# Attention and two gated layers on one core: ten zero products in front, the first pair's last keys in a bank of the fold's, w_out's first piece requested ahead of the first values

## The chip, the cores and the metric

The kernel runs on one core of a Trainium2 chip. The metric is the device time of one execution in microseconds; a time of a kernel is the median of its runs. TensorE (PE in the profile; PEld is its weight loads), VectorE (DVE), ScalarE (ACT), GpSimd (POOL) and SyncE (SP, which requests most transfers) work side by side, each through its own list of instructions in order.

## The reference

Three layers follow each other, without a non-linearity between the second and the third's first product:

```python
scores = cap * np.tanh(scale * np.matmul(q, k.transpose(0, 1, 3, 2)) / cap)
attn = np.exp(scores - np.max(scores, axis=-1, keepdims=True))
attn = attn / (np.sum(attn, axis=-1, keepdims=True) + 1e-09)
x = np.matmul(attn, v)                 # 4 batches, 12 heads, 448 tokens, 64 wide
...
h = (x @ w1) * (x @ w2) @ w3 @ w_out   # 1792 x 768, 768 x 1024, 1024 x 1024, 1024 x 768
...
h = h @ w_in                           # 768 x 1024
e = np.exp(h - h.max(-1)); solu = h * e / (e.sum(-1) + 1e-09)
out = ((solu - mean) / np.sqrt(var + 1e-06) * g_ln) @ w_out2
```

The weights of the second and third layer arrive in 64-bit floats; q, k, v and the weights as the kernel multiplies them are 32 bits wide.

## The kernel before

Two heads make a pair; there are 24 pairs, numbered from 0. A pair's 448 keys are cut into four chunks: chunks 0 to 2 of 128 keys for each head, and chunk 3, "the last keys", 64 keys of both heads in one. `scores` (L237) multiplies keys by queries into a PSUM tile of two banks, tag `sc0` or `sc1`, one buffer each; `exps` (L254) applies tanh in place and exp into SBUF (tile `p`) on ScalarE; `values` (L276) multiplies `p` by the values into the two banks of `o`. Pair 0 is scored with plain 32-bit products (two passes of an instruction for each half of the operands); from pair 1 on queries and keys are split by `split_pair` (L210) into a rounded part and a rest (`qh`, `ql`, `kh`, `kl`) on VectorE and scored in three products. The values of pairs 0 to 3 are used whole.

Beside this runs the *fold*: w3 @ w_out @ w_in is multiplied out once (`fold`, L368), first w_out by w3 (tile `f`, two buffers, tag "f"; L378). Its operands come through `Ahead` (L51): a list of pieces of 512 KB, each requested on SyncE (`landing`, L150, three landing buffers `ld`), turned from 64 to 32 bits in three VectorE operations (`convert`, L163: L168, L169, L170, into one of two buffers `cv`), and split by a ScalarE cast (L174) and a VectorE subtraction (L175). A landing buffer is free when the third operation has read it. The first pieces are w_out's chunk 0 in two halves (`in_wo`, tile `w_o_0`), then four of w3 (`in_w3t`; `w_0_0` to `w_0_3`), then w_out's chunks 1 to 5 in halves.

At the start (L655 to L679) SyncE requests the cap, then pair 0's queries, keys and values (`load_pair`, L189), then as many pieces as there are landing buffers, then pair 1's queries, keys and values. TensorE has nothing to multiply yet; `WARM` = 12 products of a tile of zeros (L663) fill the time, into a bank of tag "f". In the first turn of the loop over pairs (g = 0, phase 0) pair 0's chunks 0 and 1 are scored into `sc0` and `sc1`; six more zero products follow (L701); the last keys are scored into `sc0` again, once chunk 0's exponential has read it. The loop takes the chunks' exponentials in the order of L708:

```python
for turn, x in enumerate((run[0], (n + phase, 3), run[1])):
```

that is chunk 0, last keys, chunk 1. `ahead.step` (L719) puts the next piece's conversion beside them. The order in which instructions then stand on each engine is made by a scheduler from the program's order, priorities and its own estimate of times; on the chip each engine follows its list and waits where an operand isn't there. Names of the trace leave out pair numbers: `sc_3` or `p_3` of the order rows is chunk 3, `o_0` and `o_1` are the heads, a further number is a buffer's.

Of the kernel before, what the change touches and what calls it, by code (L numbers as in the profile page):

```python
# [10 lines left out]
F32 = mybir.dt.float32  # L11
# [8 lines left out]
P = 128  # L20
B, H, S, D = 4, 12, 448, 64
# [5 lines left out]
HALF = 512  # L27
# [8 lines left out]
NV = 2 * (NCH - 1) + 1  # L36
FILL = 4600
W3 = 9
WARM = 12
LANDS = 3  # L40
PASSES = ((0, 1), (2, 3))
NOP = 9
# [8 lines left out]
class Ahead:  # L51
# [9 lines left out]
    def loads(self):  # L61
        while self.loaded < len(self.items) and self.loaded < self.at + self.depth:
            _, load, _, _, _, there = self.items[self.loaded]
            if there is not None and not there():
                return
            load()
            self.loaded += 1

    def step(self, n=1):

# [28 lines left out]
def attention_moe_solu(ctx: ExitStack, tc: tile.TileContext, q, k, v, cap, w12, w3t, wo, win, wout2, g_ln, out):  # L99
# [9 lines left out]
    pe, act, dve, pool, sync = nc.tensor, nc.scalar, nc.vector, nc.gpsimd, nc.sync  # L109
# [34 lines left out]
    ps = ps_cm.__enter__()  # L144


    ahead = Ahead(LANDS)
# [38 lines left out]

    landed, ready, parts, outs, xr, stored, inv = {}, {}, {}, {}, {}, set(), [None]

    def load_pair(n):  # L189
        if n == 1:  # L190

            kd, qd = (at.tile([P, 2, S], F32, tag="hi", bufs=4, name=f"{x}d{n}").rearrange("p a s -> p (a s)")[:, :w] for x, w in (("k", HALF), ("q", S)))
        else:
            qd = at.tile([P, S], F32, tag="qd", name=f"qd{n}")
            kd = at.tile([P, HALF], F32, tag="kd", name=f"kd{n}")
        for t, src in ((qd, q), (kd, k)):
            sync.dma_start(out=t, in_=src[n])
        if n in PLAIN:
            vd = at.tile([P, 2, S], F32, tag="lo", bufs=4, name=f"vf{n}").rearrange("p a b -> p (a b)")
            vd = vd[:, :NV * (D + 1)].rearrange("p (c d) -> p c d", c=NV)  # L200
            pool.memset(vd[:, :, D:], 1.0)
            sync.dma_start(out=vd[:, :, :D], in_=v[n])
        else:
            vd = at.tile([P, NV, D], F32, tag="vd", name=f"vd{n}")
            sync.dma_start(out=vd, in_=v[n])
        landed[n] = qd, kd, vd
        if not n:
            ready[0] = qd, None, kd, None, vd
# [26 lines left out]
    tiled = [None, None]  # L235

    def scores(n, c, place_):  # L237

        qh, ql, kh, kl = ready[n][:4]
        sc = ps.tile([P, 2, HALF], F32, tag=f"sc{place_}", name=f"sc{n}_{c}")  # L240
        terms = ((kh, ql), (kl, qh), (kh, qh)) if n else ((kh, qh),)
        for m, (kk, qq) in enumerate(terms):
            keys = kk[:, c * P:(c + 1) * P]
            if c == 3:
                pe.matmul(sc[:, 0, :S], keys, qq, start=(m == 0), stop=(m == len(terms) - 1))
                continue
            for j in range(2):
                rows = slice(j * D, (j + 1) * D)
                tiled[0] = pe.matmul(sc[:, j, :S], keys[rows], qq[rows, :], start=(m == 0), stop=(m == len(terms) - 1))  # L249
        return sc  # L250
# [402 lines left out]


    sync.dma_start(out=capt, in_=cap.to_broadcast([P, 1]))  # L655
    load_pair(0)
    if WARM:

        zero = at.tile([P, 2, S], F32R, tag="hi", bufs=4, name="zero")
        dve.memset(raw(zero[:, 0]), 0.0)  # L660
        idle = ps.tile([P, HALF], F32, tag="f", bufs=2, name="idle")
        for i in range(WARM):
            pe.matmul(idle[:, :S], zero[:, 0, :P], zero[:, 0], start=True, stop=True)  # L663
# [25 lines left out]
    for g in range(NP // 2):  # L689
        n, first, at_once = 2 * g, g % 2, 2 * g in PLAIN  # L690
        for phase in range(3):
            run = (((n, 0), (n, 1)), ((n, 2), (n + 1, 0)), ((n + 1, 1), (n + 1, 2)))[phase]
            one, two = (first, 1 - first) if phase != 1 else (1 - first, first)
            with tc.high_priority():
                tiles = [scores(*run[0], one)]
                with tc.issue_after(tiled[0].ins):
                    tiles.append(scores(*run[1], two))
            if not g and not phase:
                with tc.issue_after(tiled[0].ins):
                    for i in range(WARM // 2):  # L700
                        pe.matmul(idle[:, :S], zero[:, 0, :P], zero[:, 0], start=True, stop=True)  # L701
            if phase:
                last_keys(n + phase - 1)
            if not at_once and (phase or n > len(PLAIN)):
                if not phase:
                    tiled[1] = tiled[0]
                behind(*(((n - 1, 1), (n - 1, 2)), ((n, 0), (n, 1)), ((n + 1, 0),))[phase])
            for turn, x in enumerate((run[0], (n + phase, 3), run[1])):  # L708
                if turn == 1:
                    if phase == 2:  # L710
                        continue
                    with tc.high_priority():
                        sc = scores(*x, one)
                else:
                    sc = tiles[turn // 2]
                split_scores(*x, exps(*x, sc))
                if g or phase:
                    with tc.issue_after(exp_[0, 1].ins) if not g else nullcontext():
                        ahead.step(2 if g >= NP // 4 else 1)  # L719
# [37 lines left out]
    ps = ps_cm.__enter__()  # L757
# [116 lines left out]
    a = operands(0)  # L874
# [3 lines left out]
    for n in range(PAIRS):  # L878
# [5 lines left out]
        if not last:  # L884
            a = operands(n + 1)
            if n + 2 < PAIRS:
                load_ab(n + 2)
        else:
            load_wg(1)
            a = turned_operands(0, tps)  # L890
# [7 lines left out]
    for n in range(PAIRS):  # L898
# [5 lines left out]
        if not last:  # L904
            a = turned_operands(n + 1, tps)
# [58 lines left out]
```

## Time and profile before

| | |
|---|---|
| median of 3 runs | 836.03 us (836.0 to 838.24) |
| the profiled execution | 837.27 us, its span 835.5 |
| TensorE busy, of the span | 819.0 us, 98% |
| VectorE, ScalarE, GpSimd | 586.2 (70%), 478.4 (57%), 74.8 (9%) |
| weight loads | 682.9 us (82%) |
| moved by DMA | 173.48 MB, mean 208 GB/s |

Instructions of one line of the kernel, engine and operand names form a group; a time in brackets at the end of a timeline's row is how long the engine had been idle before it, with what ended that. TensorE's busy time holds some waiting, since the products' ends are modelled: where a stretch is of interest, its products' starts are to be compared. Times are counted from the span's start.

### The profile page before, as it was taken

To read this page: it belongs to the slowest core of one execution; us is meant where nothing else is said; L and a number is where in the kernel's file an instruction comes from. 1 tells how busy PE (TensorE), PEld (TensorE's weight loads), DVE (VectorE), ACT (ScalarE), POOL (GpSimd) and SP (SyncE) were. 2 spreads that over 40 slices of the span, in tenths; PEclk is the share of its full clock that TensorE was granted. 3 is DMA by queue.
4 is the path that set the end of the run, shared out by engine and by line. 5 is a ranking of instruction groups with operands and counts; after the bars stand their busy time and mean duration, and the time that the engine had idled before them with its cause. 6 is when DMAs were issued, how large, how long until landed. Compare 5 with 4: busy or idle time off the path is not lost.

```text
span 835.5 us, 12215 instructions
## 1 busy us (share of the span) xinstructions
PE 819.0 (98%) x4363; PEld 682.9 (82%) x4363; DVE 586.2 (70%) x1048; ACT 478.4 (57%) x739; POOL 74.8 (9%) x149
## 2 busy tenths in 40 slices
PE   8999999999999999999899999999999999999998
PEld 4657888866777888887779899998888888999997
DVE  6889968878875787778855452433987877995452
ACT  6767868778677877765752220212555656763341
POOL 1110110110311221111111000000000000000000
PEclk9999999999999999999999999999999999999999
DMA  7878645578977355688677999983533325844211
GB/s 239 273 240 275 209 150 157 175 222 280 277 263 206 114 183 184 207 269 274 198 232 259 347 381 346 360 287 102 184 113 115 100 101 186 264 156 152 89 64 75
DMA packets 95645, 173.48 MB, mean 208 GB/s; under 512 B 13280, under 2 KB 66272, under 8 KB 93536
## 3 DMA queue, kind: packets, MB, share of 16 engines
q1 hardware_dynamic: 90592, 161.51, 57.5%
q0 software_dynamic: 4992, 11.19, 5.4%
q8 instruction: 34, 0.56, 0.3%
q14 instruction: 27, 0.22, 0.1%
HBM read 116.40 MB, written 50.68 MB: 200 GB/s over the span
## 4 chain that ended last, share of the span: by engine, by line
PE 70%; DVE 11%; DMA 11%; ACT 4%; issue 3%; SPq 0%; POOL 0%; DVEq 0%; POOLq 0%; ACTq 0%
PE ab L604 20%; PE u L766 16%; PE v L766 8%; PE o L290 6%; PE f L396 6%; PE f L378 5%; PE y L766 4%; DMA wg_dr<-cv 3%; PE sc L249 3%; DVE cv L169 2%; DMA ld<-in_wo 2%; DVE cv L170 2%; PE tp L836 1%; DVE cv L168 1%; DVE lo L273 1%
## 5 line engine op out<-in xcount | busy, mean ns | idle before, releaser
L604 PE MATMUL ab<-xs,wt 128*128 128x448 f32 x1152 | 241.7, 366 | 2.5 <-DVE abs L612 1.6
L604 PEld LDWEIGHTS ab<-xs,wt 128*128 128x128 f32 x1152 | 216.0, 188 | 23.9 <-DVE abs L612 2.0
L257 ACT ACTIVATE sc<-sc,qscale 128x896 f32<-128x896 f32 (+1 forms) x96 | 84.9, 884 | 34.8 <-PE sc L249 26.4
L258 ACT ACTIVATE p<-sc,capt 128x896 f32<-128x896 f32 (+1 forms) x96 | 85.6, 916 | 1.5
L290 PE MATMUL o<-hi,v 128*66 128x448 f32 (+1 forms) x360 | 84.7, 371 | 0.8 <-ACT x L306 0.6
L766 PE MATMUL u<-ws,a 128*128 128x512 f32 x336 | 82.1, 394 | 0.0
L378 PEld LDWEIGHTS f<-w,w_o 128*128 128x128 f32 x576 | 72.7, 191 | 10.5 <-issue 5.9
L378 PE MATMUL f<-w,w_o 128*128 128x256 f32 x576 | 78.5, 289 | 1.4 <-DVE w_o L175 0.9
L766 PEld LDWEIGHTS u<-ws,a 128*128 128x128 f32 x336 | 62.8, 187 | 14.8
L273 DVE TENSOR_TENSOR lo<-p,hi 128x896 fp32r<-128x896 f32 x60 | 64.9, 1084 | 9.7 <-ACT hi L269 9.5
L396 PE MATMUL f<-w_i,w 128*128 128x512 f32 x288 | 70.2, 393 | 1.1 <-DVE w L175 0.8
L608 ACT COPY a<-ab 128x448 f32<-128x448 f32 x32 | 17.0, 532 | 88.4 <-PE ab L604 84.1
L766 PE MATMUL u<-wg,c 128*128 128x384 f32 x336 | 65.4, 340 | 0.0
L396 PEld LDWEIGHTS f<-w_i,w 128*128 128x128 f32 x288 | 53.7, 188 | 14.3 <-DVE w L175 1.2
L168 DVE TENSOR_SCALAR cv<-ld 128x512 uint32<-128x512 uint32 (+1 forms) x80 | 32.8, 413 | 41.8 <-DMA wg_dr<-cv 25.3
L290 PEld LDWEIGHTS o<-hi,v 128*66 128x66 f32 (+1 forms) x360 | 39.1, 135 | 26.1 <-issue 9.1
L766 PEld LDWEIGHTS u<-wg,c 128*128 128x128 f32 x336 | 58.3, 188 | 0.1
L269 ACT CAST hi<-p 128x896 fp32r<-128x896 f32 x60 | 56.6, 947 | 0.4
L612 DVE TENSOR_TENSOR abs<-ab,a 128x448 f32<-128x448 f32 x32 | 19.9, 621 | 48.5 <-PE ab L604 41.3
L169 DVE SCALAR_TENSOR_TENSOR cv<-ld,cv 128x512 uint32<-128x512 uint32 (+1 forms) x80 | 52.1, 659 | 0.8
L170 DVE SCALAR_TENSOR_TENSOR cv<-ld,cv 128x512 uint32<-128x512 uint32 (+1 forms) x80 | 52.1, 658 | 0.7
L290 PE MATMUL o<-lo,v 128*66 128x448 f32 x120 | 42.6, 367 | 2.4 <-DVE lo L273 2.3
(132 smaller groups left out, 1237.4 us busy)
## 6 DMA issues: line engine op xcount, KB each, us to landing
ld<-in_w SPq DMA_DIRECT2D x24, 512.0 KB, 4.3
w_dr<-wt SPq DMA_DIRECT2D x8, 1536.0 KB, 6.5
wt<-w_dr SPq DMA_DIRECT2D x8, 1536.0 KB, 8.8
ld<-in_w3t SPq DMA_DIRECT2D x16, 512.0 KB, 4.4
ab_dr<-abs SPq DMA_DIRECT2D x32, 224.0 KB, 4.9
ldab<-ab_dr SPq DMA_DIRECT2D x14, 512.0 KB, 3.9
c_dr<-e SPq DMA_DIRECT2D x14, 512.0 KB, 2.6
ldc<-c_dr SPq DMA_DIRECT2D x14, 512.0 KB, 3.6
```

The source lines that it names most:

```text
L168: dve.tensor_scalar(x, hi, 5, 2, ALU.logical_shift_left, ALU.logical_shift_right)
L169: dve.scalar_tensor_tensor(x, hi, 0xC0000000, x, ALU.bitwise_and, ALU.bitwise_or)
L170: dve.scalar_tensor_tensor(x, lo, 29, x, ALU.logical_shift_right, ALU.bitwise_or)
L257: act.activation(sc[:, :w, :S], sc[:, :w, :S], AF.Tanh, scale=qscale)
L258: exp_[n, c] = act.activation(p, sc[:, :w, :S], AF.Exp, scale=capt)
L269: act.copy(hi, p)
L273: dve.tensor_tensor(lo, p, raw(hi), ALU.subtract)
L290: product_.append(pe.matmul(outs[n, j][:v_.shape[-1], :S], v_, t[rows, j if c < 3 else 0], **flags))
L378: pe.matmul(f[:, :QW], lw[:, a], rw[:, e], start=(g == 0 and m == 0), stop=(g == NF - 1 and m == 2))
L396: pe.matmul(f, w34[:, a, c, :], rw[:, e], start=(c == 0 and m == 0), stop=(c == NC - 1 and m == 2))
L604: pe.matmul(pp[f, b, i][:, :S], w[:, u], xs[b, c][:, e], start=(c == 0 and m == 0), stop=(c == NC - 1 and m == 2))
L766: pe.matmul(bank, a[m][:, x, k * P:(k + 1) * P], wb[m][:, e, k, :], start=(first and k == 0 and i == 0), stop=(k == NF // 2 - 1 and i == 2 ...
```

## The change

Ten zero products stand in front, not twelve, and the six behind the first scores are gone. In the first turn the last keys of pair 0 are scored into the second buffer of tag "f" instead of `sc0`, behind chunk 1's scores, and their tanh and exponential come behind chunk 1's, not ahead of them. `Ahead.first` requests the first piece of w_out; `load_pair(0)` calls it behind the keys and ahead of the values.

```diff
-WARM = 12
+WARM = 10
...
+    def first(self):
+        self.items[0][1]()
+        self.loaded = 1
...
-    def load_pair(n):
+    def load_pair(n, between=lambda: None):
...
         for t, src in ((qd, q), (kd, k)):
             sync.dma_start(out=t, in_=src[n])
+        between()
         if n in PLAIN:
...
-        sc = ps.tile([P, 2, HALF], F32, tag=f"sc{place_}", name=f"sc{n}_{c}")
+        if place_ is None:
+            sc = ps.tile([P, HALF], F32, tag="f", bufs=2, name=f"sc{n}_{c}").rearrange("p (a s) -> p a s", a=1)
+        else:
+            sc = ps.tile([P, 2, HALF], F32, tag=f"sc{place_}", name=f"sc{n}_{c}")
...
-    load_pair(0)
+    load_pair(0, ahead.first)
...
-            if not g and not phase:
-                with tc.issue_after(tiled[0].ins):
-                    for i in range(WARM // 2):
-                        pe.matmul(idle[:, :S], zero[:, 0, :P], zero[:, 0], start=True, stop=True)
...
-            for turn, x in enumerate((run[0], (n + phase, 3), run[1])):
-                if turn == 1:
-                    if phase == 2:
-                        continue
-                    with tc.high_priority():
-                        sc = scores(*x, one)
-                else:
-                    sc = tiles[turn // 2]
+            turns = [(run[0], tiles[0]), ((n + phase, 3), None), (run[1], tiles[1])]
+            if phase == 2:
+                turns.pop(1)
+            elif not g and not phase:
+                turns[1:] = turns[:0:-1]
+            for x, sc in turns:
+                if sc is None:
+                    with tc.high_priority(), tc.issue_after(tiled[0].ins) if not (g or phase) else nullcontext():
+                        sc = scores(*x, one if g or phase else None)
```

The scheduler's lists change well beyond these lines, down to some 185 of TensorE's 1454 rows. At the start of TensorE's list there stood before:

```order
L663 MATMUL idle<-zero 128x448 x12
L249 MATMUL sc_0_156<-qd_99,kd_100 128x448 x2
L249 MATMUL sc_1_159<-qd_99,kd_100 128x448 x2
L701 MATMUL idle<-zero 128x448 x6
L245 MATMUL sc_3_171<-qd_99,kd_100 128x448
L290 MATMUL o_0_179<-p_0_168,vf_103 65x448
L290 MATMUL o_1_180<-p_0_168,vf_103 65x448
```

and now (the lines' numbers have moved):

```order
L671 MATMUL idle<-zero 128x448 x10
L257 MATMUL sc_0_154<-qd_99,kd_100 128x448 x2
L257 MATMUL sc_1_157<-qd_99,kd_100 128x448 x2
L253 MATMUL sc_3_166<-qd_99,kd_100 128x448
L298 MATMUL o_0_171<-p_0_160,vf_105 65x448
L298 MATMUL o_1_172<-p_0_160,vf_105 65x448
```

The last keys' scores (`sc_3`) follow chunk 1's directly. Further down TensorE's list, from the values of pair 0's chunk 1 on, there stood before:

```order
L290 MATMUL o_0_179<-p_1_176,vf_103 65x448
L290 MATMUL o_0_179<-p_3_173,vf_103 65x448
L290 MATMUL o_1_180<-p_1_176,vf_103 65x448
L290 MATMUL o_1_180<-p_3_173,vf_103 65x448
L245 MATMUL sc_3_206<-ql_141,kh_144 128x448
L245 MATMUL sc_3_206<-qh_140,kl_145 128x448
L245 MATMUL sc_3_206<-qh_140,kh_144 128x448
L290 MATMUL o_0_179<-p_2_197,vf_103 65x448
L290 MATMUL o_1_180<-p_2_197,vf_103 65x448
L378 MATMUL f_0_0_375<-w_0_0_273,w_o_0_213 128x256 x6
L378 MATMUL f_0_0_375<-w_0_1_285,w_o_0_213 128x256 x6
L249 MATMUL sc_1_254<-ql_141,kh_144 128x448 x2
```

and now:

```order
L298 MATMUL o_1_172<-p_1_163,vf_105 65x448
L298 MATMUL o_0_171<-p_3_168,vf_105 65x448
L298 MATMUL o_1_172<-p_3_168,vf_105 65x448
L386 MATMUL f_0_0_367<-w_0_0_265,w_o_0_205 128x256 x6
L253 MATMUL sc_3_198<-ql_139,kh_142 128x448
L253 MATMUL sc_3_198<-qh_138,kl_143 128x448
L253 MATMUL sc_3_198<-qh_138,kh_142 128x448
L298 MATMUL o_0_171<-p_2_189,vf_105 65x448
L298 MATMUL o_1_172<-p_2_189,vf_105 65x448
L386 MATMUL f_0_0_367<-w_0_1_277,w_o_0_205 128x256 x6
L386 MATMUL f_0_0_367<-w_0_2_331,w_o_0_205 128x256 x6
L257 MATMUL sc_1_246<-ql_139,kh_142 128x448 x2
```

Six fold products on w3's first piece moved ahead of pair 1's last keys, and six on its third piece ahead of pair 1's chunk 1. On VectorE, behind the conversion of w3's first two pieces, there stood before:

```order
L175 TENSOR_TENSOR w_0_0_273<-cv_227,w_0_0_273 128x512
L175 TENSOR_TENSOR w_0_1_285<-cv_276,w_0_1_285 128x512
L168 TENSOR_SCALAR cv_288<-ld_220 128x512
L168 TENSOR_SCALAR cv_342<-ld_231 128x512
L169 SCALAR_TENSOR_TENSOR cv_288<-ld_220,cv_288 128x512
L169 SCALAR_TENSOR_TENSOR cv_342<-ld_231,cv_342 128x512
L218 CAST qh_296<-qd_243 128x448
L170 SCALAR_TENSOR_TENSOR cv_288<-ld_220,cv_288 128x512
```

and now:

```order
L179 TENSOR_TENSOR w_0_0_265<-cv_219,w_0_0_265 128x512
L172 TENSOR_SCALAR cv_280<-ld_212 128x512
L173 SCALAR_TENSOR_TENSOR cv_280<-ld_212,cv_280 128x512
L174 SCALAR_TENSOR_TENSOR cv_280<-ld_212,cv_280 128x512
L179 TENSOR_TENSOR w_0_1_277<-cv_268,w_0_1_277 128x512
L223 CAST qh_288<-qd_235 128x448
L223 CAST kh_292<-kd_236 128x512
L172 TENSOR_SCALAR cv_334<-ld_223 128x512
L179 TENSOR_TENSOR w_0_2_331<-cv_280,w_0_2_331 128x512
```

The third piece is converted in one go between the first two splits; its own split stands behind the casts of pair 2's queries and keys. On SyncE the request for w_out's first piece stands ahead of pair 0's values; the 8 transfers behind are in the order of before.

## Rows read from the trace of the kernel before

**Rows 1.** The page's chain that ended last, by engine.

```profile
PE 70%; DVE 11%; DMA 11%; ACT 4%; issue 3%; SPq 0%; POOL 0%; DVEq 0%; POOLq 0%; ACTq 0%
```

**Rows 2.** The chain of waits in order of time, 0 to 60 us: start, length, what.

```profile
2.81 4.80 DMA ld<-in_wo
...
22.88 4.80 DMA ld<-in_wo
```

**Rows 3.** Timeline of TensorE, 48 to 78 us: start, length, instruction, count, idle before.

```profile
49.71 0.50 PE L378 MATMUL f<-w,w_o 128*128 128x256 f32 x2 [0.50 <-ACT e L382]
51.13 0.39 PE L378 MATMUL f<-w,w_o 128*128 128x256 f32 x1 [0.92 <-DVE w_o L175]
...
63.91 0.47 PE L249 MATMUL sc<-ql,kh 64*128 64x448 f32 x2 [0.57 <-ACT p L258]
...
77.47 0.47 PE L249 MATMUL sc<-ql,kh 64*128 64x448 f32 x2 [0.49 <-ACT p L258]
```

**Rows 4.** Busy time by stretch: engines' us and instructions, granted clock, DMA share, GB/s.

```profile
20.00:25.00 5.00, 5.00 (x30) 2.89 (x29) 4.69 (x10) 3.78 (x7) 1.89 (x3) 1.00 1.06 308
```

**Rows 5.** Timeline of TensorE, 0 to 24 us.

```profile
1.39 4.78 PE L663 MATMUL idle<-zero 128*128 128x448 f32 x12 [1.39 <-DVE zero L660]
6.11 1.77 PE L249 MATMUL sc<-qd,kd 64*128 64x448 f32 x8
7.81 1.50 PE L701 MATMUL idle<-zero 128*128 128x448 f32 x6
9.25 1.02 PE L245 MATMUL sc<-qd,kd 128*128 128x448 f32 x2
10.11 1.67 PE L290 MATMUL o<-p,vf 128*65 128x448 f32 x4
12.54 1.02 PE L249 MATMUL sc<-qd,kd 64*128 64x448 f32 x4 [0.76 <-ACT p L258]
...
14.09 3.65 PE L290 MATMUL o<-p,vf 128*65 128x448 f32 x8
...
21.40 0.47 PE L249 MATMUL sc<-ql,kh 64*128 64x448 f32 x2
```

**Rows 6.** Requests at 1.65, 2.12, 3.48 and 17.90: KB each, us to landing.

```profile
kd<-in_k SPq DMA_DIRECT2D x1, 256.0 KB, 3.6
...
vf<-in_v SPq DMA_DIRECT2D x1, 224.0 KB, 4.1
...
ld<-in_wo SPq DMA_DIRECT2D x1, 512.0 KB, 5.5
...
kd<-in_k SPq DMA_DIRECT2D x1, 256.0 KB, 4.0
```

**Rows 7.** Timeline of ScalarE, 7 to 31 us.

```profile
8.19 1.01 ACT L258 ACTIVATE p<-sc,capt 128x896 f32<-128x896 f32 x1
...
10.95 1.53 ACT L258 ACTIVATE p<-sc,capt 128x448 f32<-128x448 f32 x2
```

**Rows 8.** Timeline of VectorE, 7 to 52 us.

```profile
7.63 0.43 DVE L168 TENSOR_SCALAR cv<-ld 128x512 uint32<-128x512 uint32 x1 [3.59 <-DMA ld<-in_wo]
...
9.43 0.42 DVE L168 TENSOR_SCALAR cv<-ld 128x512 uint32<-128x512 uint32 x1
...
12.64 0.69 DVE L219 TENSOR_TENSOR kl<-kd,kh 128x512 fp32r<-128x512 f32 x1
...
17.70 1.29 DVE L175 TENSOR_TENSOR w<-cv,w 128x512 fp32r<-128x512 f32 x2
...
22.16 0.69 DVE L170 SCALAR_TENSOR_TENSOR cv<-ld,cv 128x512 uint32<-128x512 uint32 x1
...
43.02 0.62 DVE L231 CAST v<-vd 128x448 fp32r<-128x448 f32 x1 [2.25 <-DMA vd<-in_v]
```

**Rows 9.** Weight loads of the zero products and the first scores: ns min/median/max.

```profile
L663 PEld LDWEIGHTS idle<-zero x12: 288/330/333, 1.4 to 5.3; 128*128 128x128 f32 x12
...
L249 PEld LDWEIGHTS sc<-qd,kd x8: 183/186/187, 6.1 to 7.0; 64*128 64x128 f32 x8
```

## The prediction

> **What bounds the kernel now.** I read the page's chain first: it ends on TensorE for 70% of the span, with 11% each of VectorE and DMA [rows 1]. Followed in order of time, nearly all of that DMA and VectorE lies ahead of 51 us, and the first link is the transfer of w_out's first piece, requested at 2.81 and there 4.80 us later [rows 2]. From 51 us on it is TensorE almost alone. So the change can pay in one way: TensorE must stand further along in its fixed list of products when the chain goes over to it. What it can win there is bounded by its waits behind that point and by what it does with the first 20 us. The named waits are 0.50 and 0.92 us at 49.7 and 51.1, and 0.57 and 0.49 at 63.9 and 77.5 [rows 3]; from 20 us on it is busy all the time, while VectorE is busy 4.69 of 5 us and the DMA's share is full at 308 GB/s [rows 4].
>
> A measurement of this kernel can tell about 0.3% (2.5 us) from no change; the three runs alone lie 836.0 to 838.24. The sum below is made against the profiled execution, 837.27 us (span 835.5 and 1.8 around it), which is 1.24 above the median of 836.03; I move the result by the same 1.24.
>
> **The start.** The twelve zero products begin at 1.39 and the first scores at 6.11 [rows 5]: 0.39 us each. The first pair's keys were requested at 1.65 and were there 3.6 us later, at 5.25 [rows 6], so the scores waited for zero products and not for data. Ten end at 5.33, still behind the keys: **-0.78 us** for the scores. The six other products filled 7.81 to 9.25 [rows 5]; there the scores of the last keys waited for the bank of chunk 0. Now they have a bank of their own, so they follow at once: scores of three chunks, 1.70 + 0.86 us, end at 7.9. The bank is the fold's second one, first wanted by the fold's second tile, 24 products behind the first, when the exponential that reads it is long done: no cost.
>
> ScalarE's exponential of chunk 0 ended at 9.20 (8.19 + 1.01) [rows 7]; 0.78 earlier is 8.4. Its list is now chunk 0, chunk 1, two casts, last keys. The exponential of chunk 1, which ended at 12.48 behind that of the last keys [rows 7], ends some 2 us after 8.4, at 10.4. Chunk 2's scores, at 12.54 the first product that waited for it [rows 5], start near 10.4, **2.1 us earlier**. The request of the first values goes behind 512 KB more: they landed at 6.2 (2.12 + 4.1) [rows 6], the piece 1.4 later at 7.6. The two change places, so the values land at 7.6. They are read at 8.4: hidden by the exponential, with 0.8 to spare.
>
> **VectorE's chain.** The piece now lands 1.4 behind the keys, at 6.7, not 7.61. Its conversion (7.63 to 9.43 [rows 8]) ends at 8.5. But the second piece, requested at 3.48, lands at 9.0 (5.5 later [rows 6]) in both, since the bytes ahead of it are the same. So VectorE stands still for half a microsecond and the rest of its chain, unbroken to 17.7, moves up only **0.4 us**: the split of pair 1's keys from 13.33 to 12.9 [rows 8], the first fold weights' split from 17.70 + 0.69 = 18.4 to 18.0.
>
> **TensorE from 13 to 24 us.** Pair 1's first scores wait for that split of the keys and end at 13.7. Then come the values of chunk 1 and of the last keys: 3.6 us as now (14.09 + 3.65 = 17.7), or down to some 2.4 if the two products on 64 rows, now neighbours, run side by side as the 64-row scores do (four pass pairs in 1.70 us) [rows 5]. So TensorE is through at 16.1 to 17.3. In the new list the next six products are the fold's, on weights that exist at 18.0: it waits 0.7 to 1.9 us. What the start won is given back here. Then 0.8 us of fold, 0.7 of scores and 1.5 of values (as in the row at 10.11), 0.8 of fold: 21.8. The next six fold products use w3's third piece. Its conversion, put ahead of the second's split, takes 1.9 from 18.0 and the split 0.6; then VectorE waits in its list for pair 2's keys, which landed at 21.9 (17.90 + 4.0 [rows 6]) and now 0.4 earlier, and splits the piece by 22.9. TensorE waits 1.1 again, and comes to pair 1's chunk 1 at 23.7, where it was at 21.40 [rows 5]: 2.3 later, with six more fold products done (0.8): **1.5 us behind**.
>
> **What comes back.** The same reordering frees a landing buffer early. The third w3 piece was converted by 22.85 (22.16 + 0.69 [rows 8]), since two conversions were interleaved and one waited for its data; only then was the next w_out piece requested, at 22.88 [rows 2]. Now it is through at 19.9, and the request goes out near 20.0. Later pieces win less, as SyncE's list is in order and the DMA has little room from 20 us on [rows 4]; I take 1 to 2.5 us at the pieces wanted at 49 to 51 us, enough to remove the waits there: **-1.4 us**. Of the two behind them (1.06), which are ScalarE's exponentials held up behind casts, I take half: **-0.5 us**.
>
> Sum: +1.5 - 1.4 - 0.5 = -0.4; 836.9 for an execution like the profiled one, **835.6 us** beside the median. Bounds: if all idle time named went and nothing came in its place, -0.78 - 1.44 - 0.76 - 2.5 = -5.5; if the two waits stand and nothing comes back, +1.5, and with ScalarE's next delay (first rival) +2.4.
>
> **The clock.** The zero products hold TensorE busy ahead of the scores. Their weight loads took 330 ns, those of the scores behind them 186 [rows 9]: the zero products, 0.39 us for 448 columns, ran at the 1.2 GHz level (448 columns in 0.373) and the scores at 2.4. The Trainium skill (TensorE: Matmul & The Clock Gate, What's actually happening) says that the engine starts throttled and that activity releases it; by it, two products fewer speak against the change, at the price of the fourth rival. In the trace the rise falls together with the end of the twelve, which bears the rule out as far as one rise can. I take no cost, since the scores now follow without a gap and keep the engine as busy.
>
> **The rivals.**
> - *Slower: TensorE stays behind.* The fold products that now stand early hold it twice as above, and ScalarE's cast of w3's fourth piece, now ahead of a tanh, waits for VectorE to about 25.7 (four operations behind pair 2's splits), so pair 1's next exponential ends near 29.6 (two casts, two tanh, itself) and TensorE loses up to 0.9 more. It decides if the wait at 43.02, where VectorE lost 2.25 us to pair 4's values [rows 8], stays where it is: then w_out's later pieces are no earlier and the waits at 49 to 51 stay. Price +1.5 to +2.4, and 0.9 more if pair 2 meets a cast ahead of its tanh in the same way: 837.5 to 839.3, 838.4 in the middle. For it: the order of those loads on SyncE hardly moves. Against: buffers come free earlier. Chance 0.14, a good third of it beyond 0.3%.
> - *Faster: the wins pass through.* The fold's wait is short because the 64-row products do not run side by side, the third piece's split comes before pair 2's keys matter, and supply is 2.9 us ahead to the end: -2.9, 833.1. Against: VectorE has no room to catch up [rows 4]. Chance 0.18.
> - *The piece is no earlier:* the transfers in flight share the DMA, and it lands near 7.6 as before. VectorE's chain then keeps its times, +0.4 on the forecast: 836.0. Chance 0.10.
> - *The clock rises late.* Scores, last keys and the first values cost twice: some 4 us more by 13.7, of which the wait for the keys' split and the fold's wait hide the better part; at half rate through pair 0's values as well, 3 remain: 838.6. The granted clock in the first 10 us decides. Chance 0.05.
>
> **Numbers.** The forecast has 0.53: with its term of 1.4 at 0 or with all of the later waits gone it reaches 835.0 to 837.0. Faster by over 0.3% (under 833.5): most of the second rival and a little of the forecast's edge, 0.18. Slower (over 838.5): the clock, and the upper part of the first rival, 0.10. Within: 0.72, all of the third rival in it. A range of 833.2 to 838.2 leaves out about 2 in 10.
>
> **What would show it.** Scores start near 5.3; no zero product after them; chunk 2's scores near 10.4; VectorE's first conversion near 6.7 and its second at 9.0; TensorE waits for w3's first split until about 18 and for the third until about 23; the w_out piece of 22.88 is requested near 20; little or no wait at 49 to 51. I am wrong if TensorE passes 24 us ahead of where it stood, if the weight loads of the scores take 330 ns, or if a new wait of over 2 us stands between 24 and 80 us.

## The result: 0.6% slower, and the profile after

The changed kernel takes **842.2 us** (median of 8 runs, 839.65 to 845.38) against 836.7 for the kernel before beside it (median of 8; seven lie between 836.0 and 838.31, one at 2054.41). The ratio is 1.0062, 95% interval 1.0043 to 1.0081: slower by 5.5 us, outside the range of the prediction. The profiled execution is the slowest of the eight: 845.38, its span 843.6. TensorE's busy time is 819.6 us and was 819.0, so the loss is waiting and not work.

The page's chain that ended last, by engine; beside [rows 1] its shares have hardly moved, DMA up by two points and ScalarE down by two:

```profile
PE 70%; DMA 13%; DVE 11%; issue 3%; ACT 2%; SPq 1%; POOL 0%; DVEq 0%; POOLq 0%; ACTq 0%
```

TensorE's timeline of the changed kernel, 0 to 26 us (start, length, instruction, in brackets how long idle before and what ended that), which answers to [rows 5]:

```profile
1.39 3.97 PE L671 MATMUL idle<-zero 128*128 128x448 f32 x10 [1.39 <-DVE zero L668]
5.71 1.77 PE L257 MATMUL sc<-qd,kd 64*128 64x448 f32 x8 [0.35 <-DMA kd<-in_k]
7.42 1.02 PE L253 MATMUL sc<-qd,kd 128*128 128x448 f32 x2
8.90 1.69 PE L298 MATMUL o<-p,vf 128*65 128x448 f32 x4 [0.46 <-ACT p L266]
10.76 1.02 PE L257 MATMUL sc<-qd,kd 64*128 64x448 f32 x4 [0.18 <-ACT p L266]
13.30 0.47 PE L257 MATMUL sc<-ql,kh 64*128 64x448 f32 x2 [1.51 <-DVE kh L223]
...
14.62 4.26 PE L298 MATMUL o<-p,vf 128*65 128x448 f32 x8
18.81 1.12 PE L386 MATMUL f<-w,w_o 128*128 128x256 f32 x6
...
24.30 0.86 PE L386 MATMUL f<-w,w_o 128*128 128x256 f32 x5 [1.42 <-DVE w L179]
25.09 0.47 PE L257 MATMUL sc<-ql,kh 64*128 64x448 f32 x2
```

The start is won as forecast, then lost: chunk 2's scores come at 10.76 (12.54 before), pair 1's wait for VectorE until 13.30, and pair 1's chunk 1 comes at 25.09 where it came at 21.40. Six more fold products are done by then (0.8 us), so TensorE stands **2.9 us behind**.

VectorE's timeline, 7 to 24 us, beside [rows 8]:

```profile
7.50 0.43 DVE L172 TENSOR_SCALAR cv<-ld 128x512 uint32<-128x512 uint32 x1 [3.16 <-DMA ld<-in_wo]
...
9.96 0.43 DVE L172 TENSOR_SCALAR cv<-ld 128x512 uint32<-128x512 uint32 x1 [0.58 <-DMA ld<-in_wo]
...
13.28 0.69 DVE L224 TENSOR_TENSOR kl<-kd,kh 128x512 fp32r<-128x512 f32 x1
...
18.34 0.69 DVE L179 TENSOR_TENSOR w<-cv,w 128x512 fp32r<-128x512 f32 x1
...
20.25 0.69 DVE L174 SCALAR_TENSOR_TENSOR cv<-ld,cv 128x512 uint32<-128x512 uint32 x1
...
23.56 0.69 DVE L179 TENSOR_TENSOR w<-cv,w 128x512 fp32r<-128x512 f32 x1
```

TensorE again, all its named waits between 30 and 100 us, beside [rows 3]:

```profile
33.29 1.45 PE L386 MATMUL f<-w,w_o 128*128 128x256 f32 x10 [0.47 <-DVE w_o L179]
...
45.31 1.45 PE L386 MATMUL f<-w,w_o 128*128 128x256 f32 x10 [0.86 <-DVE w_o L179]
...
67.72 0.47 PE L257 MATMUL sc<-ql,kh 64*128 64x448 f32 x2 [0.33 <-ACT p L266]
...
73.21 0.98 PE L386 MATMUL f<-w,w_o 128*128 128x256 f32 x6 [1.00 <-DVE w L179]
...
76.24 0.47 PE L253 MATMUL sc<-ql,kh 128*128 128x448 f32 x1 [0.55 <-ACT p L266]
...
84.23 1.38 PE L298 MATMUL o<-hi,v 64*66 64x448 f32 x8 [0.68 <-DVE hi L281]
```

The waits of 0.50 and 0.92 at 49.7 and 51.1 are gone, but six others stand in this stretch, 3.89 us in all against 2.48 in the four rows of before. Four of the six, 3.01 us, are for VectorE's splits, two for exponentials. From some 105 us on TensorE, VectorE and ScalarE run the same instructions in the same order in both traces, so a place in the chain can be compared: the 31 fold products that follow the scores behind a block of 41 start at

```profile
123.16 3.89 PE f L378 x31
```

in the kernel before and, in the changed one, at

```profile
127.88 3.90 PE f L386 x31
```

which is 4.7 us later. The rest of this execution's 8.1 us (843.6 over 835.5) comes behind it.

### The profile page after: what moved, and what is told of

It reads as the page before. It is cut to its first block, busy times and chain, and to the rows that moved or that the text cites. A ratio compares the mean times of both kernels' runs of the same rounds, so it can differ in the third digit from the quotient of the medians.

```text
span 843.6 us, 12197 instructions
## 1 busy us (share of the span) xinstructions
PE 819.6 (97%) x4355; PEld 682.6 (81%) x4355; DVE 587.5 (70%) x1048; ACT 478.3 (57%) x739; POOL 74.5 (9%) x149
## 4 chain that ended last, share of the span: by engine, by line
PE 70%; DMA 13%; DVE 11%; issue 3%; ACT 2%; SPq 1%; POOL 0%; DVEq 0%; POOLq 0%; ACTq 0%
PE ab L612 19%; PE u L771 16%; PE v L771 8%; PE o L298 6%; PE f L404 6%; PE f L386 5%; PE y L771 4%; DMA wg_dr<-cv 4%; PE sc L257 3%; DVE cv L173 2%; DVE cv L174 2%; PE tp L841 1%; DVE cv L172 1%; DMA kd<-in_k 1%; DMA rb<-r_dr 1%
## 5 line engine op out<-in xcount | busy, mean ns | idle before, releaser
L386 PEld LDWEIGHTS f<-w,w_o 128*128 128x128 f32 x576 | 72.6, 191 | 14.5 <-issue 6.4
L386 PE MATMUL f<-w,w_o 128*128 128x256 f32 x576 | 78.5, 289 | 3.8 <-DVE w L179 2.4
L172 DVE TENSOR_SCALAR cv<-ld 128x512 uint32<-128x512 uint32 (+1 forms) x80 | 32.6, 411 | 42.5 <-DMA wg_dr<-cv 27.4
```

Of the source, the lines that this page charges most:

```text
L172: dve.tensor_scalar(x, hi, 5, 2, ALU.logical_shift_left, ALU.logical_shift_right)
L386: pe.matmul(f[:, :QW], lw[:, a], rw[:, e], start=(g == 0 and m == 0), stop=(g == NF - 1 and m == 2))
```

## Experiments

Each ran in five rounds beside the kernel before on the same chip, so ratios compare across runs better than medians. "The lists" are the orders in which the scheduler puts instructions on the engines; how many rows of them differ was counted.

| run | edits of the change in it | lists | median, us | ratio to before (95%) |
|---|---|---|---|---|
| e1_changed_again | all | the change's | 841.75 | 1.0061 (1.0040 to 1.0082) |
| e2_request_alone | request | before's | 838.24 | 1.0015 (1.0000 to 1.0030) |
| e3_bank_alone | bank, no six zeros | before's but for 5 rows | 838.38 | 1.0013 (0.9998 to 1.0028) |
| e4_request_back | all but the request | the change's | 842.40 | 1.0068 (1.0043 to 1.0093) |
| e5_twelve_in_front | all, but twelve zeros | before's but for 7 rows | 838.72 | 1.0012 (0.9990 to 1.0034) |
| e6_ten_in_front_alone | ten zeros | before's | 837.61 | 1.0000 (0.9977 to 1.0024) |
| e7_eleven_in_front | all, but eleven zeros | a third | 843.07 | 1.0075 (1.0047 to 1.0102) |
| e8_fold_held_back | all, fold held back | a fourth | 846.25 | 1.0102 (1.0073 to 1.0131) |
| e9_ten_between | none | before's to 26 us, the change's from 100 us | 842.93 | 1.0063 (1.0042 to 1.0083) |
| e10_twelve_between | none | before's | 838.22 | 1.0013 (0.9999 to 1.0027) |
| e11_cast_behind | all, one cast held back | a fifth | 848.60 | 1.0135 (1.0114 to 1.0157) |
| e12_casts_on_gpsimd | all, 14 casts on GpSimd | a sixth | 845.75 | 1.0106 (1.0074 to 1.0138) |
| e13_casts_on_gpsimd_before | none, 14 casts on GpSimd | a seventh | 841.16 | 1.0046 (1.0024 to 1.0068) |
| e14_piece_behind_exponential | all, pieces held back | an eighth | 854.19 | 1.0199 (1.0170 to 1.0228) |

### Which part of the change

e1 is the changed kernel as it is.

> The changed kernel once more, for a second profile. Three theories of the 5.5 us. The list: the fold products that now stand early hold TensorE, and nothing comes back; then the wait for w3's third split (1.6 us at 22.6 in the first profile) and TensorE some 4 us behind at 100 us are here again, and the time is 840 to 843. The request: w_out's first piece ahead of the values makes the landings behind it later; then the second piece lands at 9.9 again, not at 9.0. The clock: TensorE stands idle for 2 us ahead of pair 1's scores, and a stretch at 1.2 GHz follows in some executions; then the granted clock of 10 to 20 us differs between the two profiles, and the times spread over 4 us or more.

e2 is the kernel before with `first` and `load_pair(0, ahead.first)`.

> The kernel before with w_out's first piece requested ahead of the first values, nothing else; the lists of TensorE, VectorE and ScalarE stay those of before. The list: 836 to 837, as before. The request: the first conversion starts at 7.5 or earlier, but the second piece lands at 9.9 and VectorE's split of pair 1's keys ends at 13.9 rather than 13.3; +0.5 to +3 us. The clock: as before.

e3 is the changed kernel with these two lines back:

```diff
-WARM = 10
+WARM = 12
...
-    load_pair(0, ahead.first)
+    load_pair(0)
```

> The kernel before with the last keys in the fold's bank, behind chunk 1, and without the six zero products; twelve stand in front, the request stays behind the values, and the lists stay those of before but for these products. The list: 835.5 to 837. The request: the same. The clock: TensorE is idle for some 2 us ahead of pair 1's scores, as chunk 2's are ready 2 us earlier and the split of the keys is not; in some executions a stretch at 1.2 GHz follows; +1 to +4 us and a spread of 3 us or more.

e4 has only the second of them back.

> The changed kernel with the request behind the values again; its lists on TensorE, VectorE and ScalarE stay those of the change. The list: 840 to 843, as the change. The request: the second piece lands at 9.0, VectorE's chain is 0.6 us earlier, and the time falls to 836 to 838. The clock: 839 to 843, as the idle stretch ahead of pair 1's scores stays near 2 us.

The loss came with e1 and e4, which have the change's lists, and not with e2 and e3, which keep those of before. The request is no part of it, since e4 is as slow without; what the request or the bank costs by itself, 0.15% and 0.13%, can't be told from nothing. Two signs that had been named for the clock did come: its rows differ between the two profiles of the changed kernel, and e1's times spread over 6 us. It is not the cause all the same: stretches of e4 (behind the stretch's length TensorE's busy us; its granted clock third from the end) have the granted clock at 1.00,

```profile
12.00:15.00 3.00, 1.68 (x10) 0.75 (x9) 2.93 (x7) 2.47 (x4) 0.00 (x0) 1.00 0.91 299
15.00:19.00 4.00, 2.55 (x10) 0.64 (x8) 3.88 (x9) 1.45 (x3) 0.00 (x0) 1.00 0.19 42
```

as have all its later ones to 100 us, and it is as slow as the changed kernel, in whose profile the clock fell:

```profile
12.00:15.00 3.00, 1.45 (x7) 0.68 (x8) 2.93 (x6) 2.51 (x4) 0.00 (x0) 1.00 0.96 333
15.00:19.00 4.00, 4.00 (x9) 0.85 (x7) 3.92 (x8) 1.31 (x2) 0.00 (x0) 0.57 0.10 24
```

### The edits with the lists of before

e5 is the whole change with `WARM = 12`; e6 is the kernel before with `WARM = 10` and six zeros kept. By the scheduler's own estimate it takes both the bank and two zeros fewer to tip the order.

> The changed kernel with twelve zero products in front in place of ten; the scheduler then keeps the lists of the kernel before but for three rows of TensorE, two of ScalarE and two of SyncE. Theory 'the list' (the loss of 5 us is made by the order that the scheduler gives the fold's products and VectorE's work beside them, not by any of the three edits): 836.5 to 839.5, no wait of TensorE for w3's split at 17 to 18.8 and at 22.6. Theory 'the edits add up' (request alone and bank alone measured +0.15% and +0.13%, each within its noise): their sum, +0.28%, 839.5 and no less than 839. Theory 'the clock' (no six zeros, so TensorE idles ahead of pair 1's scores and its clock falls): 841 or more, and a fall of the granted clock near 15 to 20 us.

> The kernel before with ten zero products in front, the six behind the first scores kept, nothing else changed; lists of before. Theory 'the list': TensorE starts 0.8 us earlier and waits for VectorE's split of pair 1's keys as before, 836 to 837.5, ratio 0.999 to 1.001. Theory 'fewer zeros cost' (the clock's rise comes later or the start is disturbed): first scores' weight loads at about 330 ns, 838.5 or more.

Both are as the kernel before. In e5 TensorE reaches pair 1's chunk 1 at 21.01 (21.40 before) and has no wait for w3's splits there; its place in the chain is 121.62, 1.5 us ahead of before in the two profiles, which its median of 838.72 does not confirm as a gain. So the edits, all but the two zero products in e5 and these alone in e6, cost nothing that can be told, and win nothing.

### Other lists for the change

e7 has `WARM = 11`. e8 holds fold products back:

```diff
+    mark = {}
...
+                    after_ = mark.get({0: ("v", 0, 2), 1: ("v", 0, 2), 4: ("s", 1, 1), 5: ("s", 1, 1)}.get(g)) if fq == c == 0 else None
...
+                        with tc.issue_after(after_.ins) if after_ is not None else nullcontext():
```

(the last line around the product of L386), where `after_` is the last product of pair 0's chunk 2 values for w3's first piece and pair 1's chunk 1 scores for the third.

> The changed kernel with eleven zero products in front: 0.39 us more of zeros, but the scheduler makes a third set of lists, in which the fold's products on w3's first and third piece stand behind pair 1's chunk 2 values and pair 1's first exponentials, as before, and VectorE splits both first pieces ahead of the third's conversion. Theory 'the list, by its early fold products': idle time of TensorE up to 24 us about 2 us under that of the changed kernel, 836.5 to 839.5. Theory 'the edits': as the changed kernel, 840.5 to 843, since one zero product is all that differs. Any list that is another: open, the lists differ from before's by some 240 rows of TensorE, and 839.5 to 842 would say that it is the later part of a list that costs.

> The changed kernel (ten zeros, request in front, bank) with two conditions added: the fold's products on w3's first piece may not stand ahead of the values of pair 0's chunk 2, those on its third piece not ahead of pair 1's chunk 1 scores. VectorE keeps the changed kernel's order down to the split of w3's fourth piece. Theory 'the list, by its early fold products on TensorE': the waits at 17 to 18.8 and at 22.6 go, idle time up to 24 us 1.5 to 2.5 us under that of the changed kernel, and 837.5 to 840. Theory 'the list, by VectorE's order': the waits come back at other products of the fold behind 24 us, idle up to 40 us as in the changed kernel, 841 to 843.

Both expectations of the theory of the early fold products missed. In e7 TensorE is at pair 1's chunk 1 at 21.48 like before, and the kernel still loses 0.75%; its waits come at 27 to 37 us (0.75, 0.34, 0.32 and 0.51, for casts and splits of weights). Its 843.07 lies at the edge of the range for the theory of the edits, which e5 speaks against. e8 lies above the ranges of both its theories. In it the wait at 24 us went, but another showed ahead of it, on the last keys of pair 1:

```profile
19.48 0.74 PE L254 MATMUL sc<-ql,kh 128*128 128x448 f32 x1 [2.01 <-ACT p L268]
```

The exponential it names is late in ScalarE's list. In the changed kernel the same stands on ScalarE:

```profile
13.57 0.97 ACT L265 ACTIVATE sc<-sc,qscale 128x896 f32<-128x896 f32 x1
17.68 0.62 ACT L178 CAST w<-cv 128x512 fp32r<-128x512 f32 x1 [3.14 <-DVE cv L174]
18.21 1.00 ACT L266 ACTIVATE p<-sc,capt 128x896 f32<-128x896 f32 x1
```

The tanh of pair 0's chunk 2 is done at 14.5, and its exponential waits behind a cast of w3's first piece, which VectorE has not converted before 17.6. In the list of before the cast stands behind the exponential and the next tanh:

```profile
14.68 1.01 ACT L258 ACTIVATE p<-sc,capt 128x896 f32<-128x896 f32 x1
15.59 0.97 ACT L257 ACTIVATE sc<-sc,qscale 128x896 f32<-128x896 f32 x1
17.05 1.22 ACT L174 CAST w<-cv 128x512 fp32r<-128x512 f32 x2 [0.48 <-DVE cv L170]
```

### The list without the change, and the cast put back

e9 and e10 are the kernel before, with another number in L700: `range(10)` and `range(12)` in place of `range(WARM // 2)`. e10's lists are those of before; e9's differ from them by 70 rows of TensorE, none of them ahead of 26 us, and agree with the change's from some 100 us on, where those of before do too. e11 is the changed kernel with

```diff
-            split(th, tl, cvs.pop(i))
+            with tc.issue_after(exp_[0, 2].ins) if key == ("3", 0, 0) else nullcontext():
+                split(th, tl, cvs.pop(i))
```

> The kernel before with ten zero products in place of six behind the first scores, none of the three edits. The scheduler answers with another list: as before down to about row 31 of TensorE's (26 us), but from there on like the changed kernel's, with all of that one's tail (TensorE's rows behind 110, some 100 us on). Four zero products more cost nothing by themselves if e10, with six more and the list of before, is as before. Theory 'the early part of the list' (TensorE's fold products and ScalarE's cast of w3's first piece in front of an exponential, 14 to 24 us, cost the 5 us): 836.5 to 839, idle of TensorE at 24 us as before. Theory 'the later part' (26 to 100 us): 840.5 to 843, idle as before at 26 us and 2 to 4 us more at 80 us.

> The kernel before with twelve zero products in place of six behind the first scores; the lists of before. Control of e9. The six more take about 1.2 us and stand in front of the last keys' scores and the first values; chunk 2's scores waited 0.76 us there, pair 1's about nothing. If VectorE's split of pair 1's keys is what ends the first 14 us: at most 0.5 us slower, 837 to 839. If TensorE's own work ends them: 838 to 839.5. Either way under the changed kernel's 842; as slow as that would say that a late start of pair 1 alone costs 5 us.

> The changed kernel with one condition: ScalarE's cast of w3's first piece may not stand ahead of the exponential of pair 0's chunk 2. In the changed kernel that exponential stands behind the cast, which waits 3.0 us for VectorE's conversion (to 17.5), and ends at 19.0. Theory 'ScalarE's cast': the exponential ends near 15.5, pair 1's last keys start near 17 and not 19, and TensorE's idle time up to 24 us falls from 12.5 to between 10 and 11. Theory 'the fold's products': those move with the list here too, so no difference is expected by it. The rest of the list is a new one (some 500 rows of TensorE differ from the changed kernel's), so the whole time says only what another list costs: as before's, 836.5 to 839.5, if 14 to 24 us is all of the loss; 840 to 845 if the later part decides.

**e9 is the decisive run:** it has none of the change's edits and the early part of the list of before, and it is as slow as the changed kernel, as the theory of the later part had it. e10, with two more zero products and the lists of before, is not. TensorE's named waits in e9 from 24 to 80 us are

```profile
31.70 0.47 PE L249 MATMUL sc<-ql,kh 64*128 64x448 f32 x2 [0.40 <-ACT p L258]
...
38.86 0.47 PE L245 MATMUL sc<-ql,kh 128*128 128x448 f32 x1 [1.87 <-ACT p L258]
...
58.20 0.47 PE L249 MATMUL sc<-ql,kh 64*128 64x448 f32 x2 [0.60 <-ACT p L258]
...
67.56 0.47 PE L249 MATMUL sc<-ql,kh 64*128 64x448 f32 x2 [0.37 <-ACT p L258]
...
73.59 0.98 PE L378 MATMUL f<-w,w_o 128*128 128x256 f32 x6 [1.33 <-DVE w L175]
```

4.57 us, and the largest has the same form on ScalarE as above, with a cast of a w_out piece between a chunk's tanh and its exponential:

```profile
32.68 0.98 ACT L257 ACTIVATE sc<-sc,qscale 128x896 f32<-128x896 f32 x1 [0.25 <-PE sc L249]
37.28 0.62 ACT L174 CAST w_o<-cv 128x512 fp32r<-128x512 f32 x1 [3.62 <-DVE cv L170]
37.80 1.00 ACT L258 ACTIVATE p<-sc,capt 128x896 f32<-128x896 f32 x1
```

e10's waits in that stretch are 2.05 us:

```profile
52.69 0.39 PE L378 MATMUL f<-w,w_o 128*128 128x256 f32 x1 [0.92 <-DVE w_o L175]
...
65.23 0.47 PE L249 MATMUL sc<-ql,kh 64*128 64x448 f32 x2 [0.34 <-ACT p L258]
...
79.09 0.48 PE L249 MATMUL sc<-ql,kh 64*128 64x448 f32 x2 [0.79 <-ACT p L258]
```

The 31 fold products start in e9 and in e10 at

```profile
127.70 3.90 PE f L378 x31
...
124.78 3.89 PE f L378 x31
```

so 2.9 of the 4.8 us between their profiles (spans of 842.5 and 837.7) are there by then. Over all profiles of these lists the place parts them: 121.62 to 124.82 with those of before (the kernel before, e2, e3, e5, e6, e10), 126.47 to 127.88 with the change's and e9's (the changed kernel, e1, e4, e9).

e11 says what the early cast is worth. With the cast behind it the exponential starts at 14.64, pair 1's last keys at 17.26 (19.77 in the changed kernel) and pair 1's chunk 1 at 21.93, not 25.09, so the early loss is that cast and the fold's wait for the same conversion, one behind the other: e8 moves only the fold's products back, e11's list the cast and those on w3's first piece. The whole kernel is slower all the same, 848.6, above the ranges of both theories: its new list has the next such place further on, at 69.89 us, where TensorE waits 3.77 us for an exponential that stands behind two casts:

```profile
61.93 0.97 ACT L266 ACTIVATE sc<-sc,qscale 128x896 f32<-128x896 f32 x1
66.98 0.62 ACT L178 CAST w<-cv 128x512 fp32r<-128x512 f32 x1 [4.08 <-DVE cv L174]
68.31 0.62 ACT L178 CAST w<-cv 128x512 fp32r<-128x512 f32 x1 [0.71 <-DVE cv L174]
68.83 1.00 ACT L267 ACTIVATE p<-sc,capt 128x896 f32<-128x896 f32 x1
```

### Are the casts all of it?

e12 (the changed kernel) and e13 (the kernel before) put the first 14 casts on GpSimd; e14 is the changed kernel with each step's condition changed.

```diff
-        act.copy(th, x)
+        cast_.append(0)
+        if len(cast_) <= 14:
+            pool.tensor_copy(th, x)
+        else:
+            act.copy(th, x)
```

```diff
-                    with tc.issue_after(exp_[0, 1].ins) if not g else nullcontext():
+                    with tc.issue_after(exp_[x].ins) if g < 2 else nullcontext():
```

> The changed kernel with the first 14 casts of weight pieces on GpSimd in place of ScalarE. ScalarE then never waits for VectorE's conversion in the first 60 us; GpSimd's time for a cast of 128x512 is not in any trace so far. Theory 'casts ahead of exponentials': TensorE's waits on exponentials up to 60 us go, its idle time from 24 to 60 us is 2 to 4 us under that of e9 (7.3 us) and about that of the kernel before (6.1) or less; 836 to 840. Theory 'VectorE's order': the waits on split weights stay or grow by what the cast is slower on GpSimd, 841 to 846.

> The kernel before with the same: its first 14 casts on GpSimd. Its ScalarE already waits for VectorE's conversion in places where no exponential is wanted, so by the theory of the casts nothing is won: 837 to 839 if GpSimd's cast is about as fast, and a loss of 1 to 4 us, by waits on split weights, where it is slower. By the theory that any new list costs: 841 or more. It is the measure for e12: e12 over e13 is what is left of the list's cost with the casts away.

> The changed kernel, with each piece's step in pairs 0 to 3 put behind the exponential of the same turn of the loop (the condition that the kernel has there for the first exponential alone). The casts stay on ScalarE but fewer can stand ahead of an exponential that is due. Theory 'casts ahead of exponentials': waits of TensorE on exponentials up to 60 us under 1 us in all, 837 to 841, unless the pieces come later by it. Theory 'VectorE's order' or 'pieces late': waits on split weights in their place, 841 to 848.

Both theories are partly right. In e12 and e13 no wait of TensorE on an exponential is left between 13 and 60 us, as the theory of the casts has it. But the time does not come back: in e12 TensorE waits 3.17 us at 15.36 for pair 1's split queries and 1.53 at 26.19 for split weights, and e12 stays 4.6 us above e13. The wait at 15.36 is mostly one of VectorE's order: its list has three operations on weights (at 11.49, 12.69 and 14.08; 0.68, 0.42 and 0.68 us) ahead of the split of pair 1's queries, which in the changed kernel stand behind it. GpSimd's cast takes 0.90 us on the mean in e12 and 0.82 in e13, ScalarE's 0.6, and e13, slower than the kernel before by 0.46%, has a list of its own, so the 4.6 us compare two lists and not the casts alone. e14 moves the pieces later and is the slowest of all, over both its ranges, with waits of both kinds (1.34 and 1.56 for exponentials, 1.66, 1.65 and 2.47 for split weights). So the casts ahead of exponentials are one form of the loss and not its whole cause; waits for what VectorE has not yet split are the other, and in the changed kernel they are the larger part of the named waits from 30 to 100 us. How much each form costs there was not measured apart.

## Why the prediction was wrong

**What failed most is the last term of the sum.** "What comes back" was put at -1.9 and the forecast so at -0.4. In the profile TensorE is 2.9 us behind at pair 1's chunk 1 and 4.7 at the 31 fold products, so the term measured +1.8. The stall at 49 to 51 us did go, as forecast, but no time came back: new waits of the same kind took its place. The term ahead of it, +1.5, had the right mechanism and was too small by 1.4. I had treated the reordered list as the old one with two groups of fold products moved, and priced those. The orders of TensorE, VectorE and ScalarE changed down to some 105 us, and the new lists cost 0.5%, some 4 us: e1 over e5 with the edits there, e9 over e10 without them (by the ratios to the kernel before).

Point by point:

- *The start, -0.78 and -1.44.* Half right. Ten zeros end at 5.36, but the keys came later and the scores start at 5.71: 0.40 won and not 0.78, with 0.35 waiting for the keys. In e1, e4 and e11 the keys were there in time, and the scores start at 5.42. Chunk 2's scores won 1.78 of the 2.1. All of it goes into the wait for VectorE at 13.30, as the text had it. The first values landed at 8.7 (requested at 2.60, 6.1 to landing) and not at 7.6, just ahead of their use at 8.90; in e1, e8 and e11 the products waited 0.53 to 0.71 for them, which the wait for VectorE hid.
- *The first piece, 0.9 earlier.* Wrong; here the third rival happened. It was requested 0.7 earlier and its conversion started at 7.50, not 7.63: it landed nearly when it had before, with the values in flight behind it. Other executions with the early request put that start at 6.79 (e5, near the forecast of 6.7), 7.49 (e2) and 8.06 (e1). What they share is the second piece: forecast unchanged at 9.0, it was waited for until 9.93 to 10.27, 9.96 in the changed kernel. VectorE's chain moved **back by 0.64** (the split of the keys at 13.28, 12.64 before) where -0.4 stood. That split starts at 13.24 to 13.61 with the early request (e1, e2, e5) and at 12.64 to 13.14 without (kernel before, e3, e4, e6, e9, e10).
- *The six zero products and the bank.* Right: nothing waits for the bank, and the products are gone without a cost that e3 or e5 can tell.
- *TensorE from 13 to 24 us.* Right in kind, short in size. Its first fold products wait for w3's first split until 18.81 (18.0 forecast), those on the third piece until 24.30 (23), and it is 2.9 us behind at pair 1's chunk 1, not 1.5. The 64-row products do run side by side: in e11, at the full clock, the eight products take 2.55 us, from 14.71 to the next at 17.26 (2.4 forecast; the row of before has 3.65 [rows 5]). I had not seen the cast ahead of pair 0's exponential, which was in ScalarE's list; behind the fold's wait it cost nothing more here, as e8 shows by uncovering it.
- *The w_out request near 20.* The buffer was free at 20.94 (20.25 and 0.69), 1.9 earlier than before and a microsecond later than forecast. The wait for pair 4's values on VectorE at 43 us stayed (1.75 to 43.17; 2.25 to 43.02 before), which was the condition of the first rival.
- *The rivals.* The first one, TensorE stays behind, is what happened, and its price of 2.4, with 0.9 more, was under the measured 5.5. Its condition came, but what it drew from it did not: the waits at 49 to 51 went. Its cast of w3's fourth piece does stand ahead of a tanh and waits for VectorE, to 26.96 (25.7 forecast; ScalarE idle for 2.45), yet no named wait of TensorE follows at once; the same mechanism is what e9 and e11 show, at other places. It had a chance of 0.14. The clock's rival did not happen in the changed kernel's profile, where the scores' weight loads took 186 ns as before; it did in part in e1 and e4 (below), and the wait for VectorE hid it.
- *The signs.* None of the three signs of being wrong came: TensorE passed 24 us behind, the loads took 186 ns, and no wait over 2 us stands between 24 and 80 us. The loss is several waits of up to 1.42 us, which the signs left out.

**What stays open.** The profiles of e9 and e10 part by 2.9 us up to 128 us and by 1.9 more behind it, and the changed kernel's by 4.7 and 3.4 from that of before. The order of instructions is the same there. In the changed kernel the same 4.7 us are there at 350 us, and the rest comes mainly around two waits,

```profile
379.71 0.47 PE L253 MATMUL sc<-ql,kh 128*128 128x448 f32 x1 [1.02 <-ACT p L266]
...
441.47 0.63 PE L298 MATMUL o<-lo,v 128*66 128x448 f32 x2 [1.74 <-DVE lo L281]
```

of which the kernel before has no first and a shorter second:

```profile
432.22 0.62 PE L290 MATMUL o<-lo,v 128*66 128x448 f32 x2 [0.40 <-DVE lo L273]
```

This part varies between executions of either list: the second wait is 1.15 in e5 and 1.63 in e10, with the lists of before, and the two parts are 4.0 and 0.7 in e1. Why it varies was not settled. Nor was it shown what one place of the list is worth by itself: every edit that moved one place gave a new list for all that follows.

## What to carry to other kernels

Where a scheduler orders the work by its own estimate of times, a change has two prices: that of its edits, and that of the list that comes out. Measure them apart: hold the list and make the edits (e5), and change the list without them (e9). Here the edits with the list held cost 0.12% on the median, less than can be told from nothing, and the eight other lists that ran, five of them with a further edit that made them, lay 0.5 to 2.0% above that of before. In a new list, look on each engine for an instruction that waits for another engine and stands in front of one that is ready and on the critical chain: a cast of 0.6 us between a tanh and its exponential held ScalarE 3 to 4 us. Look as well at what stands on VectorE ahead of a split that TensorE waits for.

## What was unexpected of the hardware

The granted clock fell to the 1.2 GHz level within 15 to 19 us of the changed kernel (0.57 as the mean of that stretch), after a stretch in which TensorE was busy 1.45 of 3 us. In e4 it was busy 1.68 of 3 us and the granted clock stayed at 1.00; in e1, behind 1.11 of 3 us, it was 1.00 from 15 to 19 us and 0.66, as a mean, from 19 to 24. The fall is thus one of some executions and not of the list. It cost little here: the values at 14.62 took 4.2 us in place of some 2.6, but the fold behind them waited for its weights anyway and started at 18.81, at 18.69 in e1 and at 18.22 in e4.

The Trainium skill (TensorE: Matmul & The Clock Gate, What's actually happening) says that the throttled state is the default and that activity releases it. The fall behind a thin stretch agrees with that; the three profiles of one list show that it comes at different places, or not at all.

The rise at the start varies too, and the column of the granted clock, 1.00 in these stretches, doesn't show it. Behind ten zero products the first scores' weight loads took 186 ns (median) in the changed kernel and in e11, but 236 in e1 and 310 in e4, with 334 and 335 as the longest, the length of the zero products' loads [rows 9]. The eight score products took 2.18 us in e1 and 2.36 in e4 in place of 1.77. In e4 pair 1's scores started at 13.16 all the same, as they wait for VectorE.

While GpSimd cast a piece in e12, VectorE's cast of the queries took twice its time:

```profile
13.03 0.80 DVE L229 CAST qh<-qd 128x448 fp32r<-128x448 f32 x1
```

GpSimd's cast ran beside it from 12.84 to 13.59; the same cast takes 0.40 in the changed kernel, where GpSimd does nothing then. It was not this one alone: VectorE's L172 on 128x512 at 17.14, 19.95 and 22.76, each beside a cast of GpSimd, took 0.72 in place of 0.43, while the subtraction ahead of each (L185), beside the same casts, kept its 0.68.
